# The u tiles of a fused attention-and-mixer kernel: transposed by TensorE for eight head pairs, by SyncE's transposing transfer from the ninth on

## The chip, the cores and the metric

The kernel runs on one core of one Trainium2 chip. The metric is the device time of one execution in microseconds (us). Before the change the median of three runs is 615.04 us (613.98 to 615.18). The profile is of one execution of its own, with a span of 612.5 us from the first to the last instruction.

The engines are TensorE (PE in the profile; PEld is its loading of weights), VectorE (DVE), ScalarE (ACT), GpSimd (POOL) and SyncE (SP), which only issues transfers here. Each executes its own instructions in a fixed order and waits on semaphores for the others.

## The reference

Two layers are fused. The first is attention with a threshold: for 8 batches of 8 heads, 576 positions and 64 dimensions, only scores within `tau` of a row's maximum are kept. The second is a mixer: a low-rank product along the sequence, added to its input, and a two-layer network on the channels.

```python
scores = scale * np.matmul(q, k.transpose(0, 1, 3, 2))
thresh = np.max(scores, axis=-1, keepdims=True) - tau
scores = np.where(scores >= thresh, scores, -1000000000.0)
scores = scores - np.max(scores, axis=-1, keepdims=True)
attn = np.exp(scores)
attn = attn / (np.sum(attn, axis=-1, keepdims=True) + 1e-09)
x = np.matmul(attn, v)                    # heads side by side: 8 x 576 x 512
h = x.transpose(0, 2, 1) @ U @ V          # rank 32, along the sequence
u = x + h.transpose(0, 2, 1)
out = u + np.maximum(u @ w_ch1, 0.0) @ w_ch2     # 512 -> 2048 -> 512
```

## The kernel before

The work is cut into 32 **head pairs** (8 batches of 4). A batch's 576 positions are four full row tiles of 128 and one of 64; the fifth tiles of two neighbouring batches are put together. For one head pair the kernel does this:

1. q and k are loaded, turned by TensorE (fp32 transposes) and copied by ScalarE.
2. A **score step** is one row tile for the two heads of the pair: TensorE makes two score tiles of 128x576 in fp32, VectorE copies each out of PSUM (`weigh`) with the row minimum of the negated scores, ScalarE computes the exponential, VectorE selects and sums (`select`). There are 144 steps and 288 tiles.
3. The selected weights (bf16) are turned, most by SyncE's transposing transfer and some by TensorE, and multiplied with v.
4. The result x is narrowed to bf16 and goes through the low-rank product (`low_rank`, `spread`), VectorE adds to make u (`sum_u`), ScalarE narrows u to bf16 (`narrow_u`), and **u is turned**, because the channel network needs the 512 channels on the partitions.

When the four pairs of a batch are done, the network runs over the batch: 64 matmuls of 128x512 up (`up`), ReLU, and 64 down (`down`); the joined fifth tiles take 64 of 128x128 up and 16 of 128x512 down for two batches.

These are the lines that turn u:

```python
        def narrow_u(_):
            nc.scalar.copy(out=pr.ub, in_=bt.x[:, :, pr.cols])

        ub = done["ub", p] = add(SCA, 0.515, narrow_u, [u, got("uT_", p - 2), got("ub", p - 1)])

        def turn_u(t):
            ps = bank[t.got[0]][:, 0:256].bitcast(BF16)
            for i in range(4):
                nc.tensor.transpose(ps[:, i * P:(i + 1) * P], pr.ub[:, i, :], identb)

        deps = [ub] + (done.get(("p1", pr.b - 2), []) if pr.hp == 0 else [])
        uT_ = done["uT_", p] = add(PE, 0.23, turn_u, deps, banks=1, kind="uT")

        def copy_u(_):
            nc.scalar.copy(out=bt.uT[:, pr.hp, :], in_=bank[uT_.got[0]][:, 0:256].bitcast(BF16))

        done["uT", p] = add(SCA, 0.478, copy_u, [uT_, got("uT", p - 1)], frees=[uT_])
```

The order of the instructions isn't written by hand. Each piece of work is a task with an engine, a guessed cost and the tasks it waits for. A small scheduler in the program (`Order.run`) walks through a model of the five engines while the kernel is built, and picks at each engine among the tasks that could start soon the one of lowest rank: the modelled time at which it is ready plus an offset `OFF` by kind and phase. The network's matmuls have a rank of their own through `DUE`. Tables of such offsets were found by search. Where the model sees TensorE idle for over 0.45 us and a bank of PSUM free, it emits **fillers**, matmuls of the identity whose result nobody reads, so that TensorE's clock stays up:

```python
                n = free[0]
                while at[PE] + 0.45 < s and last[n] <= at[PE]:
                    self.filler(n)
                    at[PE] += 0.22 if at[PE] > 5.5 else 0.43
                    last[n] = at[PE]
```

A score tile stays in a ring of six buffers (`s_sb`), its exponential in another ring of six (`e_sb`):

```python
    NS = 6
    s_ring = ring("s_sb", NS, [P, S], FP32)
    e_ring = ring("e_sb", NS, [P, S])
    ...
            ex = add(SCA, 0.667, exponential, [mins[x], got("w", tiles[0] - NS)])
```

Of the kernel before, what the change touches and what calls it, by code (L numbers as in the profile page):

```python
# [68 lines left out]
P = 128  # L69
# [6 lines left out]
B, H, S, D = 8, 8, 576, 64  # L76
# [9 lines left out]
EARLY = 8  # L86
# [4 lines left out]
W1_AT = (1, 4, 6, 9, 11, 14, 16, 19)  # L91
W2_AT = (20, 21, 23, 24, 25, 26, 28, 29)

DUE = (7.75, 80, 1258.25, 220, 779.25, 421.75, 107.5, 873)

# [11 lines left out]
PE, VEC, SCA, POOL, SP = range(5)  # L107
# [20 lines left out]
class Order:  # L128
# [3 lines left out]
    LAG = (0.0, 0.07, 0.1, 0.06, 0.0)  # L132
    SLOW = (1.0,) * 5
    TO_PE = 0.15
    BEFORE = 0.45
    PATIENCE = (0, 0.2, 0.1, 0.9, 1.35)


    BEGIN = (1.2, 4.5, 0.7, 1.3, 0.7)
    LANES = 8  # L140
    SHARE = (0.6, 0.4)
    LANDING = (3.1, 1.4)
    SWITCH = {"quadrants": 0.17, None: 0.13}
    PARTS = {"S": "quadrants"}

    HOLD = (84.27, 20.8, 39.99, 23.29, 62.35, 18.34, 53.51, 0.13, 43.1)
    KEPT = ((), (0, 1, 3, 4), (0, 1, 2, 3, 4, 5))


    OFF = {  # L150
        "copy_main": (19.13, -43.29, -8.12, 1.42, -28.78, -25.28, -22.95, 51.41, -45.85),
        "copy_rest": (60.73, 4.11, 41.5, -5.4, -29.64, 13.18, -80.58, -82.36, -26.38),
        "copy_tt": (198.41, -75.7, -33.86, 48.32, 43.85, 100.62, 7.39, -22.81, -38.44),
        "copy_u": (-21.98, 23.28, 116.5, 77.07, -33.95, 19.36, 29.03, -92.86, 6.98),
        "copy_u4": (-14.02, 51.4, 17, 17.47, -40.5, -60.28, -41.34, 103.29, 7),
        "copy_w": (-55.25, -15.23, 222.13, -81.81, -37.73, 188.9, 52.5, -41.28, 57.53),
        "down": (-108.85, 30.21, -20.13, 90.15, -87.01, -79.16, -34.24, -44.29, 29.17),
        "exponential": (-31.87, -48.96, 9.03, -42.56, 174.18, 12.19, 450.6, 189.09, 141.41),
        "finish": (28.37, -76.92, -41.93, 101.63, 56.59, 2.69, -121.7, -34.02, -50.98),
        "first": (-17.99, 10.62, -38.53, 2.6, 67.74, -65.5, 2.83, -19.66, -6.62),  # L160
        "high": (66.93, -13.94, 46.69, 712.1, 60.2, 95.3, 89.97, 88.03, 39.14),
        "inverse": (-26.26, 8.92, 39.77, 95.96, 39.08, 91.45, 463.65, 19.36, 0.65),
        "join": (13.52, 6.42, 53.64, 9.45, 3.36, 1.67, -114.73, 2.82, 39.08),
        "load": (-18.74, 67.06, -50.44, 55.17, 58.64, 82.33, 125.87, 149.78, -25.84),
        "low": (-9.73, -27.81, 40.61, -12.77, 5.4, -48.88, -55.07, -5.58, -26.87),
        "low4": (41.75, 36.85, 84.8, 33.79, 11.84, -6.69, 54.93, 183.24, 6.02),
        "low_part": (34.11, -32.17, 4.8, -1.24, -37.88, -65.32, -18.36, -17.94, 32.22),
        "low_rank": (-14.94, 306.57, -9.99, 33.17, -60.48, -12.24, -11.83, -46.7, -6.24),
        "make": (7.68, -10.52, -21.46, 3.08, -3.94, 16.95, -45.27, 13.88, 128.85),
        "narrow": (-0.28, -20.88, -40.1, -70.82, 16.79, -28.72, 19.58, 6.78, 1.71),  # L170
        "narrow_u": (-40.8, 31.47, -51.68, -32.58, -91.27, -26.3, 41.16, 82.58, 150.13),
        "narrow_u4": (14.28, 67.11, -13.63, 38.96, 69.08, -15.88, 47.54, -1.08, 25.04),
        "norm": (-36.47, 20.94, 161.35, 153.52, 17.7, 32.05, 16.49, -33.48, 39.64),
        "product": (-25.78, 3.36, 107.07, 34.07, -42.31, 23.71, 434.46, 110.74, -31.94),
        "relu": (44.83, -56.9, 29.43, 68.16, -76.53, 48.16, -10.98, -65.64, 20.44),
        "rest": (8.59, -53.71, 2.63, -9.48, -11.11, -0.73, -28.87, -55.87, 44.85),
        "scores": (-93.28, 8.57, -18.04, -47.28, 8.63, -52.95, -23.78, 413.25, 12.79),
        "select": (46.36, 293.14, 35.49, 104.01, 268.55, 52.2, 72.98, 458.57, 76.64),
        "send": (-23.34, 51.64, 92.04, 28.49, 36.91, 7.91, -217.4, 116.71, -45.23),
        "spread": (-102.39, 8.5, 9.39, -103.02, -0.46, -2.66, -90.25, 41.8, -45.93),  # L180
        "spread4": (26.63, -29.14, -107.73, -80.42, 55.43, 21.3, 10.43, -96.64, -100.01),
        "spread_v": (-62.05, 41.65, -47.22, -27.41, -38.59, 71.83, -165.61, -55.1, -78.6),
        "sum_u": (-55.36, 122.9, 45.74, 86.89, 15.92, 19.31, 4.11, 28.68, 42.79),
        "sum_u4": (15.44, 21.98, -56.37, 5.74, -50.96, -32.03, -61.24, 1.51, 8.11),
        "sums": (27.18, -39.86, -41.27, 101.93, 22.18, 54.82, -48.56, -32.18, -32.56),
        "threshold": (21.67, 39.75, 57.31, -114.62, 90.56, 114.55, -29.79, 46.4, 15.18),
        "turn4": (-47.62, -15.25, -30.68, 42.71, -53.87, -22.98, 35.92, 44.06, 19.31),
        "turn_main": (34.7, -53.42, 3.16, -104.58, -21.66, 79.99, 120.4, 29.72, 83.93),
        "turn_pe": (64.97, 45.46, -130.42, 85.1, 783.71, 163.63, -9.74, -23.06, 24.73),
        "turn_rest": (-89.01, 57.73, -34.88, -49.83, -30.63, 450.94, -36.86, -120.61, -31.99),  # L190
        "turn_u": (45.94, -3.77, -33.34, -53.57, -41.76, -35.51, 29.3, 1351.91, -155.36),
        "turn_w": (27.84, 6.6, -10.51, -30.89, 13.25, 5.13, -98.42, -39.84, 75.01),
        "twin": (4.39, -28.65, 54.86, 6.83, 27.36, 37.94, -39.09, -43.19, -45.42),
        "up": (49.2, -4.95, -54.97, 27.94, 3.9, 179.31, 88.49, -14.97, -39.78),
        "values": (-4.75, -11.18, -30.87, -20.21, -89.93, -8.58, 33.05, 56.9, 16.01),
        "weigh": (16.47, -218.81, -43.72, 80.8, 58.98, -59.6, -10.99, 13.81, 42.45),
        "weights": (-138.85, 46.32, -104.74, -59.99, 22.37, -4.15, 9.01, -37.1, -40.33),
    }

    def __init__(self, nbanks, filler):  # L200
# [2 lines left out]
    def add(self, *args, **kw):  # L203
        t = Task(*args, **kw)
        t.phase = self.phase
        t.lag = 0.0 if t.dma else self.LAG[t.engine]
        t.off = self.OFF[t.fn.__name__][self.phase]
        self.tasks.append(t)
        return t

    def run(self):
# [7 lines left out]
        at = list(self.BEGIN)  # L219
        last = [0.0] * self.nbanks  # L220
        kind = None
# [15 lines left out]
        while left:  # L237
# [6 lines left out]
            for e in range(5):  # L244
# [14 lines left out]
                first = min(s for s, _ in cands)  # L259
# [4 lines left out]
            s, t = best  # L264
            e = t.engine
            if e == PE:
                n = free[0]
                while at[PE] + 0.45 < s and last[n] <= at[PE]:
                    self.filler(n)
                    at[PE] += 0.22 if at[PE] > 5.5 else 0.43  # L270
                    last[n] = at[PE]
                    kind = "fill"
                parts = self.PARTS.get(t.kind)
                if parts != self.PARTS.get(kind):
                    s += self.SWITCH[parts]
                kind = t.kind
# [42 lines left out]
def kernel(  # L319
# [44 lines left out]
    NW = 8  # L364
# [16 lines left out]
    def ring(name, n, shape, dtype=BF16):  # L381
        return [wpool.tile(shape, dtype, name=f"{name}{k}") for k in range(n)]
# [43 lines left out]
    def got(*key):  # L426
        return done.get(key)
# [173 lines left out]
    def step_tasks(p, i, slot, S_, len_):  # L601
# [30 lines left out]
        thr = add(SCA, 0.19, threshold, mins)  # L632

        for x in range(2):
            def exponential(_, x=x, e_sb=e_ring[tiles[0] % NS], s_sb=s_ring[tiles[0] % NS]):
# [5 lines left out]
            def select(_, x=x, w_sb=w_ring[n % (NW // 2)][:, x, :], e_sb=e_ring[tiles[0] % NS],  # L641
                       s_sb=s_ring[tiles[0] % NS]):
# [66 lines left out]
    def value_tasks(p):  # L709
# [135 lines left out]
                nc.tensor.transpose(ps[:, i * P:(i + 1) * P], pr.ub[:, i, :], identb)  # L845

        deps = [ub] + (done.get(("p1", pr.b - 2), []) if pr.hp == 0 else [])
        uT_ = done["uT_", p] = add(PE, 0.23, turn_u, deps, banks=1, kind="uT")

        def copy_u(_):  # L850
            nc.scalar.copy(out=bt.uT[:, pr.hp, :], in_=bank[uT_.got[0]][:, 0:256].bitcast(BF16))

        done["uT", p] = add(SCA, 0.478, copy_u, [uT_, got("uT", p - 1)], frees=[uT_])


        if not last:
# [228 lines left out]
```

## Time and profile before

| what | value |
|---|---|
| time, median of 3 | 615.04 us |
| span of the profiled execution | 612.5 us |
| granted TensorE clock | 1.000 |
| TensorE busy | 588.1 us (96%) |
| VectorE busy | 522.0 us (85%) |
| ScalarE busy | 467.6 us (76%) |
| GpSimd busy | 364.9 us (60%) |
| DMA queue with the transposing transfers (q1) | 62.6% of 16 engines' span |
| DMA queue of GpSimd (q0) | 18.8% |

Busy shares are averages over the span; what limits the kernel can differ from stage to stage, so the slices and stretches of the span are read beside them. Matmuls are pipelined: the duration of one is longer than the distance at which the next can follow, so that costs of TensorE work are taken from distances between starts. A transfer's cost has three parts: the time that its issue holds SyncE, the time from issue to landing, and its share of the 16 DMA engines.

### The profile page before, as it was taken

What the parts mean: (1) busy time and instruction counts of PE and PEld (TensorE: products, weight loads), DVE (VectorE), ACT (ScalarE), POOL (GpSimd) and SP (SyncE); (2) the same over time, 40 slices, a digit from 0 to 9 for tenths busy, and PEclk for the clock granted to TensorE, in tenths of its full rate; (3) what the DMA queues carried; (4) which work ended last, traced back from release to release, by engine and by line L of the source; (5) the groups of instructions that cost most, each with busy time, mean ns of one, the idle gap of its engine ahead of it and who ended that gap; (6) DMA issues with size and microseconds to landing.
All of it is one profiled execution on the core that took longest, in us unless ns stands there. A gap on an engine that the chain in (4) does not pass through costs nothing. (4 is left out here: it accounts for less than half of the span.)

```text
span 612.5 us, 17223 instructions
## 1 busy us (share of the span) xinstructions
PE 588.1 (96%) x6267; PEld 354.1 (58%) x6343; DVE 522.0 (85%) x1399; ACT 467.6 (76%) x983; POOL 364.9 (60%) x596
## 2 busy tenths in 40 slices
PE   7989889999999999999999999999999999999996
PEld 3446565666566655565566665556565656456553
DVE  2999997998989999899998997999998999994101
ACT  3858898998699876897789965898698977885540
POOL 7768776777777757576666665576557643323000
PEclk9999999999999999999999999999999999999999
DMA  6799999666799799868998998878887897656203
GB/s 148 119 157 164 171 159 176 128 129 145 162 165 164 135 169 172 173 129 145 178 171 141 159 166 159 164 117 156 185 145 156 140 159 143 125 93 102 46 16 70
DMA packets 209716, 87.35 MB, mean 143 GB/s; under 512 B 187744, under 2 KB 199984, under 8 KB 209632
## 3 DMA queue, kind: packets, MB, share of 16 engines
q1 hardware_dynamic: 194624, 63.15, 62.6%
q0 software_dynamic: 14048, 22.76, 18.8%
q8 instruction: 50, 0.82, 0.6%
q10 hardware_dynamic: 960, 0.34, 0.2%
q14 instruction: 34, 0.28, 0.2%
HBM read 37.90 MB, written 9.44 MB: 77 GB/s over the span
## 5 line engine op out<-in xcount | busy, mean ns | idle before, releaser
L636 ACT ACTIVATE e_sb<-s_sb,m 128x576 bf16<-128x576 f32 x288 | 218.5, 778 | 42.9 <-DVE s_sb L613 42.2
L643 DVE SCALAR_TENSOR_TENSOR w_ring<-s_sb,thr,e_sb 128x576 bf16<-128x576 f32 x288 | 238.9, 858 | 9.2 <-ACT e_sb L636 5.9
L613 DVE TENSOR_SCALAR_CACHE_REDUCE s_sb<-trio 128x576 f32<-128x576 f32 x288 | 203.1, 750 | 22.5 <-PE trio L584 20.2
L584 PE MATMUL trio<-qkT 64*64 64x288 f32 (+2 forms) x2304 | 164.2, 410 | 1.3 <-DVE x L772 0.3
L661 POOL COPY w_ring<-w_ring 128x128 bf16<-128x128 bf16 (+1 forms) x168 | 72.0, 433 | 128.8 <-DVE w_ring L643 101.7
L584 PEld LDWEIGHTS trio<-qkT 64*64 64x64 f32 x2304 | 83.3, 133 | 58.9 <-issue 7.0
L949 PE MATMUL bank<-W2b,R 128*128 128x512 bf16 x400 | 98.8, 379 | 2.1 <-DVE x L830 0.6
L455 POOL DMA_DIRECT2D qkraw<-in_q_dram x125 | 82.3, 662 | 31.0 <-PE bank L515 25.5
L455 POOL DMA_DIRECT2D qkraw<-in_k_dram x125 | 81.2, 654 | 4.7 <-issue 4.1
L949 PEld LDWEIGHTS <-R 128*128 128x128 bf16 x576 | 53.3, 98 | 53.0 <-issue 2.5
L916 PE MATMUL bank<-uT,W1b 128*128 128x512 bf16 x327 | 81.5, 380 | 0.7
L795 POOL TENSOR_TENSOR x<-x,rec 128x256 f32<-128x256 f32 (+1 forms) x84 | 63.1, 752 | 30.0 <-DVE x L788 23.0
L916 PEld LDWEIGHTS <-W1b 128*128 128x128 bf16 x512 | 47.4, 98 | 57.2 <-issue 6.3
L747 PEld LDWEIGHTS <-wT_ring 128*128 128x128 bf16 x896 | 55.5, 98 | 9.3 <-issue 4.9
L550 POOL TENSOR_TENSOR vh<-vraw_ring,vh 64x128 bf16<-64x128 f32 x64 | 55.7, 870 | 5.5 <-ACT vh L543 0.8
L906 ACT ACTIVATE R<-bank 128x512 bf16<-128x512 f32 x90 | 52.3, 601 | 4.6 <-PE bank L916 3.7
L961 DVE TENSOR_TENSOR o<-bank,x 128x512 f32<-128x512 f32 x27 | 18.5, 685 | 34.1 <-remote 20.4
L747 PE MATMUL bank<-vh,wT_ring 128*128 128x128 bf16 x608 | 43.6, 220 | 1.8 <-POOL vh L550 1.2
L629 ACT ACTIVATE thr<-m,tau_t 128x2 f32<-128x2 f32 x144 | 42.5, 297 | 0.9 <-DVE s_sb L613 0.6
L916 PE MATMUL trio<-uT,W1b 128*128 128x512 bf16 x150 | 38.6, 379 | 1.5 <-issue 0.2
L949 PE MATMUL trio<-W2b,R 128*128 128x512 bf16 x136 | 33.4, 379 | 1.1 <-DVE s_sb L613 0.8
L906 ACT ACTIVATE R<-trio 128x512 bf16<-128x512 f32 x54 | 32.3, 600 | 2.2 <-PE trio L916 1.1
(104 smaller groups left out, 749.4 us busy)
## 6 DMA issues: line engine op xcount, KB each, us to landing
out_dram<-o SPq DMA_DIRECT2D x71, 128.0 KB, 2.6
vraw_ring<-in_v_dram SPq DMA_DIRECT2D x32, 160.0 KB, 3.6
qkraw<-in_k_dram POOLq DMA_DIRECT2D x63, 80.0 KB, 4.5
qkraw<-in_q_dram POOLq DMA_DIRECT2D x62, 80.0 KB, 3.9
vraw_ring<-in_v_dram SPq DMA_DIRECT2D x32, 128.0 KB, 4.2
qkraw<-in_q_dram POOLq DMA_DIRECT2D x63, 64.0 KB, 4.0
qkraw<-in_k_dram POOLq DMA_DIRECT2D x62, 64.0 KB, 4.1
W1b<-in_moe_w_ch_dram POOLq DMA_DIRECT2D x8, 256.0 KB, 4.9
```

The lines of the kernel that those rows point to most:

```text
L455: queue.dma_start(pr.qkraw[part, to, j, :], src[:, j, of, :])
L550: nc.gpsimd.tensor_tensor(out=pr.vh[part, tiles_, :, h, :], in0=raw[part, tiles_], in1=pr.vh[part, tiles_, :, 0, :], op=ALU.subtract)
L584: mm = nc.tensor.matmul(cols[part, lo:hi], a.tT[hs, 0, rows], a.tT[hs, 1, lo:hi], start=True, stop=True)
L613: nc.vector.tensor_scalar(out=s_sb, in0=score_cols(slot, x), scalar1=-scale, scalar2=None, op0=ALU.mult, op1=ALU.min, accum_out=m[:, x:x + 1])
L636: nc.scalar.activation(out=e_sb, in_=s_sb, func=ACT.Exp, bias=m[:, x:x + 1], scale=-1.0)
L643: nc.vector.scalar_tensor_tensor(out=w_sb[:, 0:S], in0=s_sb, scalar=thr_[:, x:x + 1], in1=e_sb, op0=ALU.is_le, op1=ALU.mult, accum_out=pr. ...
L661: nc.gpsimd.tensor_copy(out=w_sb[:, xs, S:640], in_=w_sb[:, xs, 512:S])
L747: nc.tensor.matmul(av[:, 2 * a + j, :], w, pr.vh[:, kt, j, :, :], start=kt == 0, stop=False)
L795: nc.gpsimd.tensor_tensor(out=x, in0=x, in1=over_sum(part), op=ALU.mult)
L906: nc.scalar.activation(out=R2[:, fts, lo:hi], in_=bank[t.got[0]].rearrange("p (f c) -> p f c", c=hi - lo), func=ACT.Relu)
L916: nc.tensor.matmul(bank[t.got[0]], W1b[:, dt, ft * P:(ft + 1) * P], bt.uT[:, dt, :], start=(dt == 0), stop=(dt == 3))
L949: nc.tensor.matmul(ch, R2[:, ft, lo:lo + P], W2b[:, ft, :], start=(ft == 0), stop=(ft == 15))
```

## The change

From the ninth head pair on (24 of 32), u is turned by one transposing transfer from SBUF to SBUF, issued by SyncE, in place of four TensorE transposes into a PSUM bank and a ScalarE copy out of it. The aim is to take work from TensorE and ScalarE and to need one bank less often. The fifth tiles' u (`turn4`) is still turned by TensorE.

The rings change as well: seven buffers for score tiles (2,304 bytes a partition each) and four for exponentials (1,152 bytes), which is the same space. The scheduler's model gets new constants (TensorE begins at 3.34 in place of 1.2, the clock is taken to be up from 7.2 in place of 5.5, and VectorE's successive dependent tasks are 0.07 apart), and all ranks (`OFF`, `DUE`, `HOLD`) are new. So all engines' orders differ from those before in detail.

```diff
-DUE = (7.75, 80, 1258.25, 220, 779.25, 421.75, 107.5, 873)
+DUE = (461, 86.25, 1468.5, 516.25, 1049.25, 748, 134.75, 1357.5)
...
+    SELF = 0.07
+    WARM = 7.2
...
-    BEGIN = (1.2, 4.5, 0.7, 1.3, 0.7)
+    BEGIN = (3.34, 4.5, 0.7, 1.3, 0.7)
...  (all of HOLD and OFF: new numbers)
-                    at[PE] += 0.22 if at[PE] > 5.5 else 0.43
+                    at[PE] += 0.22 if at[PE] > self.WARM else 0.43
...
-                                           if a.engine != e or t.dma else 0.0) -
+                                           if a.engine != e or t.dma else self.SELF if e == VEC else 0.0) -
...
-    NS = 6
+    NS, NE = 7, 4
     s_ring = ring("s_sb", NS, [P, S], FP32)
-    e_ring = ring("e_sb", NS, [P, S])
+    e_ring = ring("e_sb", NE, [P, S])
...
-            ex = add(SCA, 0.667, exponential, [mins[x], got("w", tiles[0] - NS)])
+            ex = add(SCA, 0.667, exponential, [mins[x], got("w", tiles[0] - NE)])
...
+        def send_u(_):
+            nc.sync.dma_start_transpose(
+                bt.uT[:, pr.hp, :].rearrange("p (t r) -> p t r", t=4),
+                pr.ub.rearrange("p t c -> p (t c)"))
+
+        if p < EARLY:
+            uT_ = done["uT_", p] = add(PE, 0.23, turn_u, deps, banks=1, kind="uT")
+        else:
+            done["uT_", p] = done["uT", p] = add(SP, 1.3, send_u, deps, dma=0.9)
...
-        done["uT", p] = add(SCA, 0.478, copy_u, [uT_, got("uT", p - 1)], frees=[uT_])
+        if p < EARLY:
+            done["uT", p] = add(SCA, 0.478, copy_u, [uT_, got("uT", p - 1)], frees=[uT_])
```

What this does to the orders, counted in the built instructions:

| | before | after |
|---|---|---|
| TensorE transposes of a pair's u | 128 | 32 |
| ScalarE copies of a turned u | 32 | 8 |
| SyncE transposing transfers | 143 | 167 |
| fillers ahead of the first q transpose | 16 | 9 |
| fillers from there to the first `up` matmul | 60 | 74 |
| fillers after that | 6 | 1 |
| score steps ahead of the first `up` matmul | 25 | 25 |

More of the change, by code (lines that the diff above doesn't have):

```diff
@@ L144 @@
     PARTS = {"S": "quadrants"}
-    HOLD = (84.27, 20.8, 39.99, 23.29, 62.35, 18.34, 53.51, 0.13, 43.1)
+    HOLD = (61.76, 61.61, 6.12, 44, 94.32, 94.08, 76.76, 0.01, 9.57)
     KEPT = ((), (0, 1, 3, 4), (0, 1, 2, 3, 4, 5))
     OFF = {
[L151 to L197, printed above, removed]
@@ new lines @@
+        "copy_main": (25.53, 63.74, -194.99, 34.77, -69.14, 17.14, -324, 37.67, -35.45),
+        "copy_rest": (6.5, -40.06, -14.53, 24.12, -4.13, -20.91, -46.23, 54.32, -95.65),
+        "copy_tt": (-16.03, -64.1, 20.85, -110.66, 55.87, 62.18, -42.53, -53.37, -25.08),
+        "copy_u": (89.47, -53.33, 162.09, -74.19, 7.13, 9.51, -102.11, -20.31, -73.82),
+        "copy_u4": (-5.3, -56.82, -16.18, -6.54, 49.93, -37.52, 64.79, -22.2, -18.99),
+        "copy_w": (75.7, -4.79, -22.58, 20.52, -4.75, 68.84, -1.46, 27.15, 10.06),
@@ new lines @@
+        "down": (52.39, 32.35, 33.69, 38.82, 7.25, -27.49, 1.69, 19.34, 131.97),
+        "exponential": (61.02, 15.66, 97.71, -26.58, 23.56, 95.43, 116.8, 90.08, 11.21),
+        "finish": (-53.17, -45.71, 51.42, 30.79, -14.22, -26.29, 28.78, 16.33, -75.01),
+        "first": (-56.79, 75.89, 0.92, -55.7, 35.86, -3.48, 9.68, 53.63, 1.2),
+        "high": (-129.72, -35.78, 31.87, -6.58, 48.08, -20.33, -28.95, -46.46, 84.01),
+        "inverse": (46.71, -32.89, 54.08, 22.1, 122.91, 38.13, 143.23, 39.39, -23.27),
@@ new lines @@
+        "join": (2.19, 36.38, 69.81, -65.72, -28.72, -7.68, -26.75, 24.75, -3.5),
+        "load": (14.89, -38.6, -1.87, -55.09, 439, 169.52, 202.43, 266.17, -64.61),
+        "low": (23.82, 3.88, -45.02, 6.6, -28.12, -60.17, -87.19, -43.1, 26.46),
+        "low4": (64.5, 130.96, 545.14, -26.82, 13.94, -59.21, 35.95, 265.72, -23.85),
+        "low_part": (30.38, 13.98, -26.01, -41.71, 130.31, 109.34, -20.82, -133.07, -1.88),
+        "low_rank": (-57.69, 16.1, -2.98, 31.4, -60.74, 41.37, 38.61, 8.08, -35.05),
@@ new lines @@
+        "make": (-18.31, -192.85, -81.78, -52.29, 6.69, -18.25, 12.16, -35.09, 27.21),
+        "narrow": (5.95, 39.32, -9.64, -6.72, 1.46, 29.45, -10.31, 45.69, -47.12),
+        "narrow_u": (-45.99, -94.08, -136.7, -16.38, -46.01, -113.33, 15.29, 42.82, -0.02),
+        "narrow_u4": (2.02, -41.08, 15.16, 12.95, 69.79, 35.67, -44.1, -54.14, 56.42),
+        "norm": (60.22, 26.73, 14.75, 16.35, 28.89, -20.28, -16.45, 55.02, 19.4),
+        "product": (-38.14, -97.33, -17.17, 18.14, -78.98, 56.88, 40.12, 68.18, -110.66),
@@ new lines @@
+        "relu": (44.72, -2.34, -31.3, -83.46, 20.06, -116.77, 10.32, 4.5, -36.91),
+        "rest": (64.49, 74.43, 34.29, 18.04, -20.78, -41.41, -55.22, -17.62, 44.45),
+        "scores": (-2.16, -56.15, 42.01, -69.96, -15.23, -44.76, 4.79, -16.69, -3.93),
+        "select": (-41.99, 29.22, -2.51, 135.03, 570.07, 400.28, 184.53, 231.57, 188.34),
+        "send": (43.87, 17.75, 5.67, -19.7, -14.51, -9.84, 285.3, 70.92, -48.56),
+        "send_u": (54.83, -57.33, -16.36, 177.37, 12.48, 121.89, 19.74, 60.45, 25.84),
@@ new lines @@
+        "spread": (-216.88, 63.66, -12.54, -9.53, -23.32, -1.29, -122.3, 43.34, 63.38),
+        "spread4": (12.62, -19.59, -18, 54.22, -34.85, 61.33, -24.98, -50.63, -66.91),
+        "spread_v": (-113.69, -64.83, 6.03, 44.27, 73.51, -47.79, -27.38, 65.24, 2.79),
+        "sum_u": (-64.77, 3.32, 13.18, 117.53, -78.44, -9.21, 87.33, 127.21, -64.36),
+        "sum_u4": (-96.51, 65.77, 2.32, 38.3, 44.64, 21.12, -125.78, 37.98, 23.47),
+        "sums": (195.64, 23.57, 47.14, -31.56, 10.32, -16.1, 35.4, 4.49, -58.98),
@@ new lines @@
+        "threshold": (-37.94, -91.24, -43.1, -296.86, 94.89, 36.19, 66.3, 1.07, 12.5),
+        "turn4": (-36.19, -43.45, 5.14, 7.01, 54.44, -61.28, 52.57, 29.57, -92.54),
+        "turn_main": (0.34, 20.57, 26.79, -161.06, 126.25, -30.36, -38.23, -14.86, -5.97),
+        "turn_pe": (-0.48, -21.65, -184.33, 36.36, -95.83, 51.55, 181.65, 20.16, -43.63),
+        "turn_rest": (-5.99, -37.64, -0.75, 52.43, -6.2, -61.13, -8.69, -94.49, -32.06),
+        "turn_u": (-85.8, -3, -69.47, -45.79, 74.76, -7.02, 3.37, 12.83, 72.77),
@@ new lines @@
+        "turn_w": (45.6, -1.19, -137.3, 47.86, -48.09, 10.25, -28.07, -30.73, 72.41),
+        "twin": (32.78, -132.71, -13.72, -15.07, -38.22, -14.87, -64, 49.79, 55.76),
+        "up": (13.07, 75.42, -49.49, -57.58, 68.34, -48.43, 10.3, 58.82, 35),
+        "values": (-37.57, -25.94, -48.38, 20.3, -54.04, 26.74, 72.56, -4.07, -32.49),
+        "weigh": (-145.66, -20.29, -57.18, 79.45, -16.94, 55.31, 45.2, 33.27, 31.94),
+        "weights": (-56.28, 79.24, -10.97, 18.21, -35.76, 31.57, -73.46, 67.52, 113.68),
@@ L634, in step_tasks, with exponential, select @@
         for x in range(2):
-            def exponential(_, x=x, e_sb=e_ring[tiles[0] % NS], s_sb=s_ring[tiles[0] % NS]):
+            def exponential(_, x=x, e_sb=e_ring[tiles[0] % NE], s_sb=s_ring[tiles[0] % NS]):
                 nc.scalar.activation(out=e_sb, in_=s_sb, func=ACT.Exp, bias=m[:, x:x + 1],
                                      scale=-1.0)
-            ex = add(SCA, 0.667, exponential, [mins[x], got("w", tiles[0] - NS)])
-            def select(_, x=x, w_sb=w_ring[n % (NW // 2)][:, x, :], e_sb=e_ring[tiles[0] % NS],
+            ex = add(SCA, 0.667, exponential, [mins[x], got("w", tiles[0] - NE)])
+            def select(_, x=x, w_sb=w_ring[n % (NW // 2)][:, x, :], e_sb=e_ring[tiles[0] % NE],
                        s_sb=s_ring[tiles[0] % NS]):
@@ L847, in value_tasks @@
         deps = [ub] + (done.get(("p1", pr.b - 2), []) if pr.hp == 0 else [])
-        uT_ = done["uT_", p] = add(PE, 0.23, turn_u, deps, banks=1, kind="uT")
+        def send_u(_):
[6 more added lines that the diff above has]
+            done["uT_", p] = done["uT", p] = add(SP, 1.3, send_u, deps, dma=0.9)
         def copy_u(_):
             nc.scalar.copy(out=bt.uT[:, pr.hp, :], in_=bank[uT_.got[0]][:, 0:256].bitcast(BF16))
-        done["uT", p] = add(SCA, 0.478, copy_u, [uT_, got("uT", p - 1)], frees=[uT_])
+        if p < EARLY:
+            done["uT", p] = add(SCA, 0.478, copy_u, [uT_, got("uT", p - 1)], frees=[uT_])
         if not last:
```

## The prediction

> **What bounds the kernel now.** I read the busy shares first, then the slices, then the busy time by stretches, because 96% on TensorE is an average.
>
> ```profile
> PE 588.1 (96%) x6267; PEld 354.1 (58%) x6343; DVE 522.0 (85%) x1399; ACT 467.6 (76%) x983; POOL 364.9 (60%) x596
> ...
> PE   7989889999999999999999999999999999999996
> ...
> DVE  2999997998989999899998997999998999994101
> ```
>
> The first column of slices (15.3 us each) is a start-up; in the next five VectorE stands at 9 and TensorE falls to 8 in places; later TensorE is at 9 throughout, and VectorE runs out four slices before the end. The view by stretches says the same in numbers (first column the length, then busy time of each engine):
>
> ```profile
> 0.00:15.00 15.00, 11.52 (x68) 5.40 (x69) 4.23 (x16) 5.02 (x10) 11.86 (x24) 1.00 0.69 147
> 15.00:90.00 75.00, 68.15 (x960) 42.61 (x959) 72.79 (x200) 60.61 (x121) 56.80 (x100) 1.00 1.01 153
> 90.00:200.00 110.00, 105.63 (x1155) 66.48 (x1172) 98.00 (x268) 96.15 (x204) 81.03 (x137) 1.00 0.88 154
> 200.00:590.00 390.00, 384.97 (x4001) 231.37 (x4057) 343.53 (x913) 304.81 (x650) 215.19 (x338) 1.00 0.81 142
> 590.00:612.50 22.50, 17.82 (x90) 8.21 (x89) 3.46 (x5) 0.99 (x2) 0.00 (x0) 0.99 0.26 59
> ```
>
> From 15 to 90 us VectorE works 72.8 of 75 us: **VectorE is the bound**, and TensorE's 68 us there include fillers. The first `up` matmul starts at 91.0 us in the timeline. From there **TensorE is the bound**: it idles 4.4 us of 110, then 5.0 us of 390. The last 4.5 us are the end of the last matmul, its addition and the last transfer. So what leaves TensorE after 91 us shortens the kernel nearly one for one, and what leaves ScalarE doesn't by itself.
>
> **What the Trainium skill says.** "VectorE: DVE Perf Modes", section "The three transpose paths", gives 390 ns for a 128x128 bf16 transpose on TensorE, into PSUM, and 1309 ns by the DMA crossbar, into SBUF; it would have TensorE do it where PSUM will do. Those are latencies, and here latency is not what is paid: "TensorE: Matmul & The Clock Gate", section "Back-to-back issue gap", gives N/2.4 + 2.5 ns between isolated warm matmuls, 56 ns for N = 128, and says that the weight loads can stretch it to 81. The trace agrees with the lower one: the fifth tiles' group of four transposes at 304.50 us is followed by the next group at 304.72. The same page, section "Part 1: The HAM clock gate", says that the clock comes up after some 3.4 us of work whatever the number of matmuls; here the first filler starts at 3.34 us and the distance between fillers falls from 0.427 to about 0.215 us near 7.6 us, which agrees within a microsecond. "DMA: Bandwidth & Descriptors", section "Issuing engines are not separate DMA queues", says that all transfers share the same 16 DMA engines, so added ones can delay the others; the trace before shows those engines over 80% busy.
>
> **The change part by part.**
>
> *TensorE loses 96 transposes.* This is the row of what goes, with busy time and mean duration, and that of its ScalarE copy:
>
> ```profile
> L845 PE MATMUL bank<-identb,ub 128*128 128x128 bf16 x108 | 10.5, 220 | 0.5 <-DVE o L961 0.4
> L851 ACT COPY uT<-bank 128x512 bf16<-128x512 bf16 x27 | 15.8, 585 | 4.6 <-PE bank L845 4.5
> ```
>
> 220 ns is a latency and must not be multiplied by 96. What counts is from the group's start to the next group's start:
>
> ```profile
> 88.76 0.40 PE L845 MATMUL bank<-identb,ub 128*128 128x128 bf16 x4
> 89.00 0.39 PE L747 MATMUL bank<-vh,wT_ring 128*128 128x128 bf16 x4
> ```
>
> That is 0.24 us for a group of four. Some groups take longer, since the sequencer or the weight load had to wait for `ub` (2.2 us in 6 waits over all 32 groups, so 0.07 a group). I take 0.25 to 0.29 for each of 24 groups, all in the stretch that TensorE bounds: 24 x 0.26 = **6.2 us**.
>
> *ScalarE loses 24 copies*: 24 x 0.585 = 14.0 us of 467.6. Off the path: I count nothing, but it lets exponentials start sooner.
>
> *SyncE gains 24 issues.* Its transposing issues now:
>
> ```profile
> L667 SPq DMA_TRANSPOSE wT_ring<-w_ring x127: 1198/1354/3217, 17.7 to 554.8; - x127
> ...
> DMA to landing us min/median/max: 2.6/4.7/8.6
> ```
>
> The median of 1.35 us is for ten 128x128 blocks; for four blocks I estimate the 1.2 us minimum, so 24 x 1.2 = 29 us more issuing. SyncE has room: it waits over 300 us in all, 114.3 and 62.2 us of that in its two largest waits. *The DMA engines* move 96 blocks of 32 KB more, 3.1 MB beside the 63.15 MB of their queue, which took 62.6% of the span: by bytes an estimated 3 points on a load of 82%. I count 0 to 1 us for transfers that come later.
>
> *Latency of u.* In place of a 0.24 us turn and a 0.6 us copy the network waits about 4 us. In the middle other work lies between: another batch's matmuls. At the very end it matters: the last `spread` is followed by 8 `down` matmuls, the fifth tiles' turn, 4 `down` and the 64 small matmuls of the fifth tiles before the last 64 `up`. Those are 12 x 0.216 + 0.22 + 64 x 0.056 = 6.4 us, against 0.68 (`sum_u`) + 0.62 (`narrow_u`) + an estimated 4.2 from issue to landing + some tenths for the spread's own end and the handovers = 6. It just fits; I count 0.3 us lost.
>
> *The start.* Sixteen fillers stand ahead of the first q transpose:
>
> ```profile
> 3.34 5.77 PE L418 MATMUL trio<-identb 128*128 128x512 bf16 x16 [3.34 <-DVE identb L344]
> 8.95 0.60 PE L515 MATMUL bank<-ident,qkraw 128*128 128x128 f32 x4
> ```
>
> The last of the first q loads is issued by SyncE at about 2.4 us and lands some 3.6 us later, by 6.1; the last k piece is issued by GpSimd at 2.40 and lands by about 6.6 (4.2 median for such pieces in this window). So the transposes wait for fillers, not for data. Nine fillers at 0.427 us end at 3.34 + 3.84 = 7.2 us, before the clock is up. The transposes then start 1.75 us earlier, the first few at half clock (0.2 to 0.4 us back). What follows is bound by VectorE, which can start as much earlier: **1.4 us**.
>
> *The middle.* Both orders put the first `up` after 25 score steps, and VectorE has 44 selects against 43 done by the 50th score tile, so the stretch to 91 us should keep its length. Its 14 additional fillers fill waits for VectorE and cost nothing. The four fillers at 304.72 us, with the u turn behind them, cost 1.93 us before the next matmul at 306.65; four of five of that isn't in the sum yet, and the new order has no filler there: **1.4 us**.
>
> Sum: 6.2 + 1.4 + 1.4 - 0.3 - 0.5 (DMA) = 8.2 us. 615.04 - 8.2 = 606.8; I say **606.5 us**, as the freed banks and ScalarE take a little off TensorE's remaining waits.
>
> **Rivals.** (a) *The DMA takes the place of TensorE.* SyncE issues in order, so a `send_u` whose `ub` isn't ready holds back the weight transposes behind it. For it: landing already ranges to 8.6 us. Against: TensorE's waits for transposed weights are about 5 us in all before. If each of 24 sends cost 0.5 us, the gain would fall by 12 us: 615 to 619. (b) *VectorE becomes the bound.* It works 343.5 of 390 us between 200 and 590, so it can't take over for a gain of 8 us; only the start is its own. (c) *The four-deep ring of exponentials binds.* ScalarE may run only four tiles ahead of `select`; VectorE now waits 5.9 us for `e_sb` in all. Doubled in the first 90 us it would give back 3 us: 609 to 610. (d) *The new ranks are much better or worse than the old.* TensorE's idle time after 91 us, without the last 4.5, is only some 9.5 us, so better ranks bring at most about 5 us (601); worse ones have no such floor, but the new model's constants agree with this trace (first filler at 3.34 us), which speaks against it.
>
> **Range and chances.** The parts that I trust (6.2 and 1.4 at the start) lead to 607.4 alone; rival (d) reaches 601 to 602, rivals (a) and (c) 610 to 615. I give 601.5 to 612 eight chances in ten. 2% is 12.3 us, so faster needs under 602.7: 0.13. Slower needs over 627.3: 0.03.
>
> **What would show it.** TensorE busy near 580 us with 32 u transposes; the first q transpose at 7.2 to 7.6 us and the first score tile on VectorE some 1.4 us earlier; first `up` near 89.5 us; no `uT` wait of TensorE over 0.5 us except at the end; ScalarE near 454 us. The prediction is wrong if TensorE waits for `uT`, `wT_ring` or `wT` transfers by more than some 8 us in all, if VectorE idles for `e_sb` early, or if the first `up` comes later than before.

## The result, and the profile after

The changed kernel takes **605.45 us** (median of 4), the kernel before 615.11 us beside it; the ratio is 0.9842 (95% interval 0.9811 to 0.9872). A second comparison later gave 0.9840 (0.9809 to 0.9872). The gain is 9.7 us, and 606.5 was predicted. The total agrees, but the way to it isn't the predicted one. The two profiled executions, from which the parts below are read, are 7.6 us apart (spans of 612.5 and 604.9 us), less than the medians.

The page's busy shares and slices of the changed kernel:

```profile
PE 584.9 (97%) x6249; PEld 349.3 (58%) x6249; DVE 522.2 (86%) x1399; ACT 458.7 (76%) x959; POOL 371.8 (61%) x596
...
PE   7989789999999999999999999999999999999996
...
DVE  4869899999999999999988999999999999994101
```

VectorE's early columns fell from mostly 9 to 8, 6, 9, 8; its middle ones rose. To see what that does to the end, I cut each execution at three events: the first score tile on VectorE, the first `up` matmul, and the end of the last score matmul. Between the last two lies **the middle**: what TensorE and VectorE share. The view by stretches for the middle and for what follows it, of the kernel before (length, then busy time of TensorE, its weight loads, VectorE, ScalarE, GpSimd):

```profile
91.00:543.40 452.40, 443.64 (x4746) 268.80 (x4811) 423.63 (x1136) 370.50 (x791) 287.17 (x458) 1.00 0.87 153
543.40:612.50 69.10, 64.03 (x489) 36.51 (x493) 20.36 (x46) 30.47 (x61) 8.04 (x14) 1.00 0.32 62
```

and of the changed kernel:

```profile
94.00:537.50 443.50, 441.31 (x4802) 267.42 (x4802) 426.94 (x1140) 364.46 (x775) 295.21 (x460) 1.00 0.91 162
537.50:604.90 67.40, 62.44 (x420) 33.12 (x418) 20.18 (x45) 27.74 (x54) 6.17 (x11) 1.00 0.37 71
```

| stretch | before | after | predicted change | measured change |
|---|---|---|---|---|
| to the first score tile on VectorE | 12.1 | 10.5 | -1.4 | -1.6 |
| from there to the first `up` | 78.9 | 83.5 | 0 | +4.6 |
| the middle | 452.4 | 443.5 | -7.6, less up to 1 for the DMA engines | **-8.9** |
| after the last score step | 69.1 | 67.4 | +0.3 | -1.7 |

(us; the predicted -7.6 are the turn's 6.2 and the 1.4 at the fillers.) In the middle VectorE's idle time, length less busy time, fell from 28.8 to 16.6 us, more than TensorE's, 8.8 to 2.2. Both engines' sums give the same 8.9 us: VectorE has 3.3 us more work there and 12.2 less idle time, TensorE 2.3 less work and 6.6 less idle time. Half of VectorE's fall is in two of its waits, for score tiles and for exponentials. By the view of waits from 92 to 540 us, first before, then after, they are:

```profile
DVE s_sb L613 <- PE trio L584: 10.4, 13, 2.5
DVE w_ring L643 <- ACT e_sb L636: 5.5, 11, 0.9
...
DVE s_sb L616 <- PE trio L587: 6.0, 11, 0.8
DVE w_ring L646 <- ACT e_sb L639: 3.9, 6, 0.9
```

The middle repeats from execution to execution: it is 443.5 or 443.6 us in both executions of the changed kernel and in both of its variant with GpSimd's copies moved, and 452.3 or 452.4 us in the kernel before and its variant with nine fillers. The stretch ahead of the middle doesn't repeat so well, and its +4.6 us, from one pair of executions, is taken up again with the experiments on GpSimd's copies.

The start went as foreseen: in four executions with sixteen fillers the first score tile comes at 11.6 to 12.8 us, in ten with nine fillers at 9.8 to 11.2. The timeline of TensorE, changed kernel:

```profile
3.34 4.02 PE L421 MATMUL trio<-identb 128*128 128x512 bf16 x9 [3.34 <-DVE identb L347]
7.15 0.80 PE L518 MATMUL bank<-ident,qkraw 128*128 128x128 f32 x4
```

Then VectorE stood idle for 4.7 us at one place, by its timeline (in brackets the idle time ahead of the instruction and who ended it):

```profile
34.77 0.82 DVE L646 SCALAR_TENSOR_TENSOR w_ring<-s_sb,thr,e_sb 128x576 bf16<-128x576 f32 x1 [4.72 <-DMA wT_ring<-w_ring]
```

VectorE wants to overwrite a weights buffer that a transposing transfer still reads. GpSimd's and SyncE's timelines say why that is late:

```profile
24.92 1.38 POOL L664 COPY w_ring<-w_ring 128x128 bf16<-128x128 bf16 x7
...
25.31 4.95 SPq L670 DMA_TRANSPOSE wT_ring<-w_ring  x3
```

The transfers wait for GpSimd's doubling of the last 64 columns (`twin`). Seven of these copies are done in one go at 24.9 us, behind eight loads of q and k, V's copies and U's loads. In the kernel before, the same timelines have the first copy and the first transfer 7.5 us earlier:

```profile
17.39 0.29 POOL L661 COPY w_ring<-w_ring 128x128 bf16<-128x128 bf16 x1 [0.76 <-DVE w_ring L643]
...
17.71 7.30 SPq L667 DMA_TRANSPOSE wT_ring<-w_ring  x3
```

The new transfers themselves are as expected. From the view of the tile `uT`, duration of the issue (min/median/max) and time to landing:

```profile
L854 SPq DMA_TRANSPOSE uT<-ub x24: 1188/1222/1476, 184.2 to 564.7; - x24
...
DMA to landing us min/median/max: 2.4/3.1/7.7
```

TensorE's matmuls waited 5.1 us in all for transposing transfers, those of weights. Among those who waited for `uT`, no TensorE matmul of the network stands behind a transfer; the fifth tiles' small matmuls at the end cover the last one.

### The profile page after: what moved, and what is told of

It reads as the page before. It is cut to its first block, busy times and chain, and to the rows that moved or that the text cites. A ratio compares the mean times of both kernels' runs of the same rounds, so it can differ in the third digit from the quotient of the medians.

```text
span 604.9 us, 17115 instructions
## 1 busy us (share of the span) xinstructions
PE 584.9 (97%) x6249; PEld 349.3 (58%) x6249; DVE 522.2 (86%) x1399; ACT 458.7 (76%) x959; POOL 371.8 (61%) x596
## 5 line engine op out<-in xcount | busy, mean ns | idle before, releaser
L798 POOL TENSOR_TENSOR x<-x,rec 128x256 f32<-128x256 f32 (+1 forms) x84 | 69.6, 831 | 37.1 <-DVE x L791 28.9
L963 PE MATMUL bank<-W2b,R 128*128 128x512 bf16 x368 | 90.2, 379 | 0.4 <-ACT qkT L524 0.3
L930 PE MATMUL bank<-uT,W1b 128*128 128x512 bf16 x320 | 77.8, 379 | 0.7 <-ACT R L920 0.4
L930 PE MATMUL trio<-uT,W1b 128*128 128x512 bf16 x192 | 48.1, 379 | 0.2 <-DVE s_sb L616 0.2
L963 PE MATMUL trio<-W2b,R 128*128 128x512 bf16 x208 | 47.5, 379 | 0.0
L975 DVE TENSOR_TENSOR o<-bank,x 128x512 f32<-128x512 f32 x23 | 15.8, 688 | 32.1 <-PE bank L963 31.9
L746 PE MATMUL bank<-vh,wT_ring 128*128 128x64 bf16 x176 | 33.9, 193 | 0.0
```

Source lines behind the costliest of these rows:

```text
L798: nc.gpsimd.tensor_tensor(out=x, in0=x, in1=over_sum(part), op=ALU.mult)
L930: nc.tensor.matmul(bank[t.got[0]], W1b[:, dt, ft * P:(ft + 1) * P], bt.uT[:, dt, :], start=(dt == 0), stop=(dt == 3))
L963: nc.tensor.matmul(ch, R2[:, ft, lo:lo + P], W2b[:, ft, :], start=(ft == 0), stop=(ft == 15))
```

## The experiments

The prediction's theory (A) is that TensorE's work is what the middle lasts for. All kernels but two hold the order of every engine as the scheduler made it: the scheduler's picks were put in a list, and only the list was edited before the instructions were emitted. So nothing moves except what an edit names. Line numbers differ from kernel to kernel because of the edits. Ratios are to the kernel before on the same chip, with 95% intervals; us are medians. Waits are those from 92 to 540 us.

### The turn alone, in the old order

```diff
         def turn_u(t):
+            if p >= EARLY:
+                nc.sync.dma_start_transpose(
+                    bt.uT[:, pr.hp, :].rearrange("p (t r) -> p t r", t=4),
+                    pr.ub.rearrange("p t c -> p (t c)"))
+                return
 ...
         def copy_u(_):
+            if p >= EARLY:
+                return
```

> The kernel before with its order held on every engine, old ranks and old rings; only the 24 turns of u from the ninth pair on are exchanged: four TensorE transposes and a ScalarE copy go out, one SyncE transposing transfer comes in at the place of the transposes. Theory A (TensorE bounds the time after the first up matmul, and the turn is worth 24 x 0.26 us there): about 609 us, 6 us under the kernel before. Rival B (the transfers' latency and SyncE's order take the place of what TensorE gave up): 613 to 619 us. Rival C (the gain of the change comes from the new ranks, and 24 turns lie in TensorE's waits): within 1.5 us of the kernel before.

Measured: 615.07 us, ratio **1.000** (0.9983 to 1.0016). The middle by stretches:

```profile
95.50:548.10 452.60, 439.90 (x4665) 264.92 (x4730) 423.73 (x1138) 361.65 (x772) 287.84 (x459) 1.00 0.93 159
```

That is 0.2 us longer than before. The second kernel leaves the 24 turns out without a replacement (both functions only return), so its later batches work on stale u:

> The kernel before with its order held; the 24 turns are left out and nothing comes in their place, so the channel network of batches 2 to 7 works on stale u. This is the turn's whole cost in TensorE, ScalarE and PSUM. Theory A: 608.5 to 609 us, no more than 1 us under the run with transfers, so that the transfers cost next to nothing. Rival B: 2 us or more under the run with transfers.

Measured: 613.93 us, ratio 0.9975 (0.9960 to 0.9989). The middle of this one:

```profile
92.20:543.90 451.70, 439.67 (x4665) 265.11 (x4730) 423.57 (x1136) 361.23 (x771) 286.57 (x458) 1.00 0.86 153
```

This is the central reading. 96 transposes and 24 copies are gone (80 and 20 of them from the middle), ScalarE works 9.3 us less there than before, TensorE is busy 4.0 us less, and the middle is 0.7 us shorter. VectorE's idle time is 28.1 us, where it was 28.8, and its largest wait is the same one, 10.4 us in the kernel before:

```profile
DVE s_sb L622 <- PE trio L593: 10.2, 12, 2.8
```

Theory A fell, in this order. Rivals B and C both allow 615.07 us; that leaving the turns out brings only 1.1 us more speaks for C. What TensorE gave up became TensorE's own waiting: it idles 12.0 us in the middle, where it idled 8.8. What the transfers cost is the difference of the two runs: 0.25% or 1.5 us by the times, whose intervals overlap a little, and 0.9 us in the middle by the traces. 0 to 1 was expected.

### Nine fillers in the old order

```diff
+        cut = [i for i, ev in enumerate(events) if not isinstance(ev, Task)][:7]
+        return [ev for i, ev in enumerate(events) if i not in cut]
```

> The kernel before with its order held, only the first 7 of the 16 fillers ahead of the first q transpose left out. Theory A (the start waits for fillers and VectorE bounds what follows): first score tile on VectorE about 1.5 us earlier, first up matmul about 1.4 us earlier, 613.7 us in all. Rival (the earlier start is lost to a wait for loads or to the slow clock before the first up matmul): 615 us.

Measured: 612.94 us, ratio 0.9952 (0.9934 to 0.9971), so 1.8 to 4.1 us. The start theory holds in direction; its one trace shows the first score tile and the first `up` 0.9 us earlier, less than the times say. The first transposes ran on the slow clock here: four of them took 1.06 us, against 0.60 in the kernel before.

### The turn back to TensorE, in the new order

At the place of each transfer in the changed kernel stand the four transposes and the copy again, in a PSUM bank that the scheduler's model has free.

```diff
-            nc.sync.dma_start_transpose(...)
+            ps = bank[t.got[0]][:, 0:256].bitcast(BF16)
+            for i in range(4):
+                nc.tensor.transpose(ps[:, i * P:(i + 1) * P], pr.ub[:, i, :], identb)
+            nc.scalar.copy(out=bt.uT[:, pr.hp, :], in_=ps)
```

> The changed kernel with its order held, but u of the last 24 pairs turned by TensorE and copied by ScalarE again: at the place of each SyncE transfer stand four TensorE transposes into the bank that has been free longest and one ScalarE copy. With the kernel before and the run that exchanges only the turn this makes the square of old and new order by old and new turn. Theory A (in the new order TensorE has no gaps left, so the turn costs its full time): 6 us over the changed kernel, 611 to 612 us. Theory G (TensorE's and VectorE's handovers set the length of the middle in either order, and short groups go into gaps): at most 1.5 us over the changed kernel, 605 to 607 us.

Measured: 619.38 us, ratio **1.0078** (1.0051 to 1.0104). That is beyond both theories: the turn that was worth nothing in the old order is worth 14 us here. The middle is 457.7 us, 14.2 more than in the changed kernel. Two waits of ScalarE, which stands at each copy until TensorE is through, come to 15.8 us, and TensorE's matmuls wait 4.8 us for PSUM banks that these copies still read, of which this is the largest part:

```profile
ACT uT L869 <- PE bank L868: 9.4, 7, 2.2
ACT uT L869 <- PE trio L868: 6.4, 11, 1.1
PE bank L543 <- ACT uT L869: 3.4, 5, 0.7
```

Perhaps the copies only stood badly. So in the next kernel each stands two ScalarE instructions later, or directly ahead of its bank's next use if that comes first, with the bank chosen whose next use is furthest away:

```diff
+                ev.got = [max(ev.was, key=soonest)]
+                waiting.append([LATER, ev, soonest(ev.got[0])])
```

> As the run of the new order with TensorE's turn, which took 14 us more than the changed kernel and in which ScalarE waited 17.7 us at its 24 copies: here each copy stands two ScalarE instructions later, or directly ahead of the bank's next use where that comes first, and the bank is the one of the free ones that is used again last. Theory I (the 14 us come from ScalarE's waits at badly placed copies and from banks taken away, not from TensorE's 6 us of work): 610 to 613 us. Theory J (TensorE has no gaps left in the new order and any work on it costs more than its time): 617 us or more.

Measured: 620.41 us, ratio 1.0071 (1.0042 to 1.0099), and again a middle of 457.6 us. ScalarE's two waits fell from 15.8 to 9.9 us without any gain, so theory I fell. By the view of the tile `uT` (us, times):

```profile
  PE bank L913: 8.4, 6
  PE trio L913: 1.5, 3
```

TensorE's waits for these copies' banks, by contrast, grew to 6.7 us.

### What TensorE's and ScalarE's share is worth in the new order

24 fillers of 0.216 us in the changed kernel, one beside each transfer:

```diff
+            if t.fn.__name__ == "send_u":
+                spare = [n for n in range(self.nbanks) if last[n] <= at[PE]]
+                events.extend(spare[:1])
```

> The changed kernel with its order held and 24 more filler matmuls of 0.216 us (5.2 us in all), one at the place of each SyncE transfer of u, into a free bank; nothing waits for their results. Theory A: 4.5 to 5.5 us over the changed kernel. Theory G: under 1.5 us over it.

Measured: 607.77 us, ratio 0.9884 (0.9859 to 0.9909), 2.6 us over the changed kernel by the two ratios, though the intervals overlap. The traces agree: the middle is 446.4 us, 2.9 more than in the changed kernel. 21 of the 24 fillers lie in the middle, an estimated 4.5 us (21 x 0.216), and cost over half of that, so neither theory's number. And with ScalarE work in place of TensorE's:

```diff
         def send_u(_):
+            for half in range(2):
+                nc.scalar.copy(out=spare, in_=pr.ub[:, 2 * half:2 * half + 2, :])
             nc.sync.dma_start_transpose(...)
```

> The changed kernel with its order held and SyncE's transfers kept; at the place of each of the 24 transfers ScalarE has two copies of 128x256 bf16 more, from u to a spare buffer that nobody reads (about 0.68 us a pair, 16 us in all). Theory A, as in the prediction (ScalarE is off the path, it works 76% of the span): within 1.5 us of the changed kernel. Theory K (in the new order ScalarE's exponentials stand between VectorE's two passes, and its 14 us are part of what the change brings): 3 us or more over the changed kernel, so 608.5 us or more.

Measured: 609.73 us, ratio 0.9908 (0.9878 to 0.9939), some 4 us over the changed kernel, and a middle of 446.8 us, 3.3 more: theory K in its size. ScalarE, busy 76% of the span, is on the path in the new order. It isn't there by the link that theory K named: VectorE's waits for exponentials are 3.9 us in the changed kernel and 4.1 us here. Another line of VectorE's waits grew: v is split into two bf16 parts, and ScalarE copies the product with the low part out of PSUM into x, to which VectorE adds the product with the high part. VectorE waits for this copy. The lines are, in order, of the kernel before, the changed kernel, the one with copies added and the one with TensorE's turn:

```profile
DVE x L788 <- ACT x L784: 3.9, 7, 2.1
DVE x L791 <- ACT x L787: 0.8, 3, 0.5
DVE x L801 <- ACT x L797: 5.5, 13, 0.8
DVE x L803 <- ACT x L799: 8.7, 17, 1.1
```

### Each half with an order of its own

Two kernels let the scheduler work again. With the changed kernel's own offsets for the exchanged tasks the scheduler came, in both, to a point at which no task could start; so these tasks have plain offsets here. The first has the old ranks and rings with the transfer as a task:

```diff
-        uT_ = done["uT_", p] = add(PE, 0.23, turn_u, deps, banks=1, kind="uT")
+        if p < EARLY: ...
+        else:
+            done["uT_", p] = done["uT", p] = add(SP, 1.3, send_u, deps, dma=0.9)
```

> The kernel before with its ranks, rings and model, but the transfer of u as a task of its own from the ninth pair on (offset 0 in all phases), so that the scheduler makes a new order that knows of TensorE's freed time. That order has 99 fillers against 82, and as much useful TensorE work behind the last score step as before (63.7 against 64.0 us by the measured distances). Theory A: 607 to 610 us, as TensorE has 6 us less to do. Theory G (freed time pays only if network matmuls from behind the last score step move into it; here fillers took it): 614 to 618 us.

Measured: 618.11 us, ratio 1.0047 (1.0032 to 1.0062), at the upper edge of theory G. Its middle is 453.0 us. The second has the new ranks and rings with TensorE turning all of u:

```diff
-        if p < EARLY:
+        if True:
             uT_ = done["uT_", p] = add(PE, 0.23, turn_u, deps, banks=1, kind="uT")
```

> The changed kernel's ranks, rings and model, but u of all 32 pairs as a TensorE task with a ScalarE copy, scheduled anew (offset -50 for the turn and 50 for the copy, the first pair of plain values with which the scheduler comes to an end). That order has 126 fillers against 84. Theory A: 611 to 613 us. Theory H (the tables were searched for one set of tasks, and any other set loses what the search had won): 612 to 620 us, with more idle time of VectorE in the middle than the 16.6 us of the changed kernel.

Measured: 630.66 us, ratio 1.0229 (1.0199 to 1.0260), with 34.1 us of VectorE's idle time in a middle of 461.7 us: slower than even theory H said. Neither half is a gain by itself: tables of ranks that were searched for one set of tasks lose with another. Their poor results tell of an order that wasn't searched for as much as of the half.

### GpSimd's copies at the start

The changed kernel with the first seven copies directly behind their selects:

```diff
+        early = [ev for ev in events if isinstance(ev, Task) and ev.fn.__name__ == "twin"][:7]
+        for ev in early:
+            events.remove(ev)
+            events.insert(max(events.index(d) for d in ev.deps) + 1, ev)
```

> The changed kernel with its order held, except that the first seven copies of GpSimd's own (the doubling of the 64 last columns, which every transposing transfer of weights waits for) stand directly behind their selects instead of behind the loads of the next pairs and of U. Theory D (the changed kernel's 4.7 us wait of VectorE at 30 us comes from these copies, which start at 24.9 us there and at 17.4 us in the kernel before; VectorE bounds this stretch, so the end moves as well): no wait of VectorE over 1 us near 30 us, first up matmul near 89.5 us, 601 us in all. Rival E (the DMA engines are too busy with weights and loads there, so that the transfers land late anyway): VectorE waits 2 us or more at the same place, 603.5 to 605.5 us. Rival F (TensorE had enough other work, so that a gain at the start comes back as a wait later): first up matmul earlier, but under 1.5 us gained in all.

Measured: 604.23 us, ratio 0.9805 (0.9777 to 0.9833). SyncE's first transfers start 8.2 us earlier, and the 4.7 us wait is gone; the longest of VectorE's waits from 25 to 50 us are now these:

```profile
27.40 0.76 DVE L629 TENSOR_SCALAR_CACHE_REDUCE s_sb<-trio 128x576 f32<-128x576 f32 x1 [1.03 <-PE trio L600]
...
41.23 0.82 DVE L659 SCALAR_TENSOR_TENSOR w_ring<-s_sb,thr,e_sb 128x576 bf16<-128x576 f32 x1 [0.99 <-DMA wT_ring<-w_ring]
...
48.60 0.28 DVE L788 TENSOR_TENSOR x<-bank,rec 64x128 f32<-64x128 f32 x1 [1.91 <-PE bank L759]
```

The first `up` comes at 91.6 us and the end at 604.2, where theory D had 89.5 and 601. So it holds for the wait, but not for what the wait is worth.

As the interval touches that of the changed kernel, both ran once more side by side:

> The changed kernel once more, on the same chip as the next one: 605 to 606 us, the wait of VectorE of 4 to 5 us near 30 us again (if it is the order of GpSimd and not an accident of the one profile).

> The changed kernel with the first seven of GpSimd's copies moved ahead, once more and side by side with the changed kernel. Theory D (the early wait is worth what the first up matmul moved in its trace, 2.4 us): 602.5 to 604 us, the two intervals apart or nearly so. Rival F (the gain at the start comes back as a wait): both within 1 us.

Measured: 605.12 us, ratio 0.9840 (0.9809 to 0.9872), and 603.33 us, ratio 0.9823 (0.9782 to 0.9864). The changed kernel waited 5.03 us at the same place again. Four more kernels above have the changed kernel's order on every engine ahead of the first `up`, and they waited 3.0, 3.4, 4.3 and 4.4 us there. So the wait comes from this order, and moving the seven copies removes it.

What the wait costs is another matter. This is the time from the first score tile to the first `up` in every execution with one of these orders, on several chips:

| order ahead of the first `up` | us |
|---|---|
| old (four kernels) | 78.9, 79.0, 79.4, 83.9 |
| new (six executions of five kernels) | 79.3, 79.5, 79.7, 80.7, 83.0, 83.5 |
| new, GpSimd's copies moved (two executions) | 78.4, 80.4 |

With the wait, four executions needed no more than 80.7 us, and the old order once needed 83.9 us without it (this is the run with the turn alone exchanged). Two of the long ones had a lower granted clock: 0.83 from 30 to 50 us in the changed kernel's second execution, 0.91 from 40 to 60 us in the old order's. The changed kernel's first execution had 1.00 throughout and a second wait of VectorE, 2.1 us at 74.7 us. So the +4.6 us of the table further above lies within the spread of single executions and can't be put down to the new order; the means of the first two rows are 0.6 us apart. What the early copies gain, 1 to 2 us by the times, isn't settled either: the intervals overlap.

## Why the prediction was right, and where it was not

- **The start** (-1.4): right. -1.6 in the trace; the fillers alone brought 1.8 to 4.1 us by the times and 0.9 us in the trace.
- **The turn, 24 x 0.26 = 6.2 us**: this step failed, though the total came out. TensorE's groups of u transposes fell from 36 to 12 as foreseen, and leaving them out took 4.0 us from its busy time in the middle, 0.20 for each of the 20 groups there, where 0.26 was taken. What failed is the step from work to time: it was "what leaves TensorE after 91 us shortens the kernel nearly one for one". In the old order it shortened nothing (ratio 1.000), and left out altogether 1.5 us. In the new order the turn costs 14 us. The 1.4 us for the fillers at 304.72 us rest on the same step and were not tried by themselves. The square of four kernels (ratio, then the middle in us) shows that no share belongs to the turn or to the order alone:

| | old order | new order |
|---|---|---|
| u turned by TensorE | 1; 452.4 | 1.0078; 457.7 |
| u turned by SyncE | 1.000; 452.6 | 0.9842; 443.5 |

- **The middle stretch as a whole** (-7.6 before the DMA's part, -8.9 measured): near in size, by another way, so the agreement of the total is in part luck. Before, TensorE was 98% busy there and VectorE 94%: 423.6 of 452.4 us. The prediction saw VectorE's 343.5 of 390 us, rival (b), and read it as room; but those 390 us contain the last 50, in which VectorE has little left to do. That two engines so full, which hand score tiles to each other in a fixed order, have no single bound is argued from this and not shown: no run took work from VectorE alone. Shown is that TensorE's and ScalarE's work for the turn didn't set the length in the old order, and that in the new one added work on either does.
- **ScalarE off the path**: wrong in the new order. 16 us of copies put back cost 4 us. Its busy time fell by 8.9 us where 14.0 were expected, and in the kernel with the 24 turns left out by 11.2 us, 0.47 for each copy: the mean of 585 ns includes overlap with the neighbour.
- **From the first score tile to the first `up`** (0): about right, as far as executions that scatter by 4 to 5 us tell. "The first `up` comes later than before" was named as what would prove the prediction wrong. It came at 94.0 and 94.2 us in the changed kernel's two executions, in place of 91.0, but at 89.4 to 91.1 us in four kernels of the same order up to there, and at 95.5 us in one of the old order. A single pair of traces can't decide this sign. Comparing VectorE's order was not enough, though: the new order's wait of 3 to 5 us comes from GpSimd's, from seven instructions that had moved behind other work.
- **Rival (a)**, SyncE's queue: no TensorE wait for u grew, and the 5.1 us of its matmuls' waits for transposing transfers stay under the 8 named as a sign. The transfers together cost 0.9 to 1.5 us in the old order, 0 to 1 was expected. **Rival (c)**, the four-deep ring: ScalarE waits 4.2 us for `select` in the middle of the changed kernel, VectorE never for `e_sb` ahead of it; the ring wasn't tried by itself. **Rival (d)**, the new ranks: nearest to what happened, but its limit of 5 us didn't hold: TensorE's idle time in the middle alone fell by 6.6 us, and between the two kernels whose u TensorE turns the new order loses 5.3 us in the middle.

Which of the new numbers (`OFF`, `DUE`, `HOLD`, the model's constants, the rings) made the better middle stays open: taken singly they give another order that was never searched, as the two kernels with half of the change show. Why 24 turns cost 14 us in the new order is settled in part. In the middle ScalarE's copies alone cost 3.3 us and TensorE's time alone 2.9; the other 8 come only with both, and with the PSUM bank that neither run took. TensorE's waits for these banks, 4.8 and 6.7 us, may be part of it; no run tried the bank by itself.

## What to carry to other kernels

Where two engines were both over 90% busy in the stretch that counts, and their orders were fixed, removing work from one was not a gain but an offer to the order. So look at the other engine's idle time in that stretch too, without the tail, and expect the gain from an order that was searched for the new set of tasks; an order that was only made anew with old tables lost here. Leaving the work out altogether, with nothing in its place, is the quickest test of what it is worth. Take a stretch from event to event (first `up`, last score) rather than in round microseconds, then a gain of one and a loss of another can't hide each other, and take it from several executions before a cause is sought: the middle repeated within 0.2 us here, the stretch ahead of it scattered by up to 5. In a new order compare the small engines too: seven short copies of GpSimd, moved behind loads, made VectorE wait 3 to 5 us.

## What the runs showed of the hardware that was not expected

How long a transposing transfer holds SyncE hardly depended on its size: 1.22 us for four blocks of 128x128, 1.37 for the weights' transfers, most of ten blocks. Its landing did depend on it, with 3.1 us against 4.4 (all medians of the changed kernel). And the clock's rise isn't tied to a fixed time: after the same nine fillers from 3.34 to 7.15 us the next four transposes took 0.80 us in one execution and 1.06 in another, against 0.60 at the full clock, and the same sixteen fillers of the old start took 5.28, 5.77, 5.79 and 6.45 us in four executions.
